# The norm's broadcasts as fp32r products of a high and a low part

## The chip, the core and the metric

The kernel runs on one core of a Trainium2 chip. The core has five engines with instruction streams of their own: PE (TensorE, matrix products, with its weight loads shown apart as PEld), DVE (VectorE), ACT (ScalarE), POOL (GpSimd) and SP (SyncE, which here only starts transfers). Each engine takes its instructions in order, and waits for another engine by semaphores. The metric is the device time of one execution in microseconds.

## The reference

One layer of three parts, on 2 batches of 768 tokens with a width of 512:

```
def _moe_ref(x, g_ln, w_ch1, w_ch2):
    mu = np.mean(x, axis=-1, keepdims=True)
    var = np.mean((x - mu) ** 2, axis=-1, keepdims=True)
    xn = (x - mu) / np.sqrt(var + 1e-06) * g_ln
    ch = np.maximum(xn @ w_ch1, 0.0) @ w_ch2
    return (x + ch).astype(np.float32)
...
def reference(**kwargs):
    attn_out = _attn_ref(**attn_kwargs)
    x = np.ascontiguousarray(attn_out.transpose(0, 2, 1, 3)).reshape(B, S, H * D)
    x = _moe_ref(x=x, **moe_kwargs)
    return _moe2_ref(x=x, **moe2_kwargs)
```

`_attn_ref` is a retention over 8 heads of 64 with a decay per head, `_moe_ref` the norm and a two-layer perceptron with 2048 hidden units, `_moe2_ref` a causal attention with 4 experts of which each token keeps two. All inputs and outputs are float32.

## The kernel before

The activations stand transposed in SBUF as `xT`: 128 partitions, 4 groups of features, 1536 tokens. The tokens are cut into 12 chunks of 128 for the retention, and into 4 blocks of 384 (`NBLK`, `TB`) for the norm and the perceptron.

**The order of the work.** PE's order is written out by hand for the whole program. Until the call `by_hand.close()` the orders of DVE, ACT, POOL and SP are written out by hand too: this stretch holds the retention, the norm, the decoding of the first eight pieces of weights and the first steps of the perceptron (the first 110 us or so). After it a scheduler with costs of its own orders the other engines.

**The hand-written loop** (L615) goes over `n`. An iteration issues, for the retention: scores of the next chunk (`sc`, PE), state and output products (`po`, PE), decay of the next chunk (`a` on DVE, `kd` on ACT and POOL), the new state (`st` on DVE, `old` on POOL), the scaled queries (`qd` on POOL) and the copy of the chunk's output into `xT` (ACT). Behind these it issues one step of the norm for each block that is ready, then a piece of decoding or of the norm (`room`), then the evictions of one perceptron step.

**The norm of a block** has five steps, one or more iterations apart.

- `ln_a`: sums over features by four fp32 products (`mu`), then a copy from PSUM to SBUF on ACT (`mus`).
- `ln_b`: an fp32 product with a matrix of constants (`mean<-mus,part_w`) adds the four part sums and gives the mean to all partitions. DVE subtracts it (`dq`, L425), ACT multiplies by the gain into the high part of `xn` (L427), DVE makes the low part (L431), ACT squares (L433).
- `ln_c`: the same sums over the squares (`va`, then `vas`).
- `ln_d`: the variance as a column per 128 tokens (`var`), ACT's square root (`std`, L459), DVE's reciprocal (`rs`, L461).
- `ln_e` and `x2_split`: `columns` gives a column of 128 values to all partitions, by a product whose stationary operand is the column repeated and whose moving operand is the identity (L448); DVE multiplies `xT` by it. `ln_e` does this for the standard deviation (`sb`), `x2_split` for its reciprocal (`rb`).

The perceptron multiplies a high and a low part: a value is written as fp32r in two tiles, and three passes (high by high, low by high, high by low) give the product. The function `split` (L200) makes such parts: ACT casts to the high part, DVE subtracts it from the source. Products in fp32r are one instruction each; an fp32 product shows as two records in the trace.

The weights come as words of 64 bit and are decoded by a chain of DVE and ACT operations per piece (L214 to L241); the last is DVE's L241, which writes the low part of `w`. A perceptron step is `h` (L485, 12 products of 384 columns), `y` (L519) or, for the first block, `yf` (L538).

Four PSUM slots of one bank (`ps_mid`) serve `mu`, `mean`, `va`, `var`, `h`, `sb` and `rb` in turn.

Of the kernel before, what the change touches and what calls it, by code (L numbers as in the profile page):

```python
# [8 lines left out]
F32 = mybir.dt.float32  # L9
F32R = mybir.dt.float32r  # L10
BF16 = mybir.dt.bfloat16
I32 = mybir.dt.int32
U32 = mybir.dt.uint32
AF = mybir.ActivationFunctionType
ALU = mybir.AluOpType
AX = mybir.AxisListType

P = 128
B, H, S, D = 2, 8, 768, 64
HP = H // 2  # L20
# [5 lines left out]
TB = 384  # L26
NBLK = B * S // TB
NTB = TB // P
# [32 lines left out]
MASKED = -1e9  # L61
# [6 lines left out]
def model(ctx, tc, qkT, kv, lam, g_ln, w12, wat, out):  # L68
    nc = tc.nc
# [4 lines left out]
    const = ctx.enter_context(tc.tile_pool(name="const", bufs=1))  # L74
# [7 lines left out]
    lnp = mp.enter_context(tc.tile_pool(name="lnp", bufs=2))  # L82
# [3 lines left out]
    rc = rp.enter_context(tc.tile_pool(name="rc", bufs=1, side="right"))  # L86
    r2 = rp.enter_context(tc.tile_pool(name="r2", bufs=2, side="right"))
# [4 lines left out]
    def ps_mid(name):  # L92
        return psum.tile([P, 512], F32, tag="mid", bufs=4, name=name)
# [1 line left out]
    ps_one = ps_mid  # L95


    zeros = const.tile([P, 512], BF16, tag="zeros", name="zeros")
    nc.vector.memset(zeros, 0.0)

    def warm(n, name):
        ps = ps_mid(f"warm{name}")
        for _ in range(n):
            nc.tensor.matmul(ps, zeros[:, :P], zeros, start=True, stop=True)

    warm(WARM[0], "a")

# [2 lines left out]
    def ret_load(b, c, part=None):  # L110
        if part != 1:
            qk = r2.tile([P, 2, HP, P], F32, tag="qk", name=f"qk{b}{c}", bufs=3)
            nc.sync.dma_start(qk, qkT[b, c])
            R[b, c] = dict(qk=qk)
        if part != 0:
            kvn = r2.tile([P, 2, H, D], F32, tag="kvn", name=f"kvn{b}{c}", bufs=3)
            nc.sync.dma_start(kvn, kv[b, c])
            R[b, c]["kvn"] = kvn
# [54 lines left out]
    while rest:  # L173
        for p in rest:
            ft, i = p
# [24 lines left out]
    def split(dst_hi, dst_lo, src):  # L200
        nc.scalar.copy(dst_hi, src)
        nc.vector.tensor_tensor(dst_lo, src, dst_hi.bitcast(F32), ALU.subtract)
# [57 lines left out]
    qpow = rc.tile([P, HP, P], F32, tag="qpow", name="qpow")  # L260
    lq = rc.tile([P, H], F32, tag="lq", name="lq")
    dec = rc.tile([P, H, P], F32, tag="dec", name="dec")
    hit = rc.tile([P, P], F32, tag="hit", name="hit")
    order = [(b, c) for b in range(B) for c in range(NC)]
    by_hand = ExitStack()
    by_hand.enter_context(tc.manual_schedule(engines={
# [23 lines left out]
                                qpow[:, :, m - 1:m].to_broadcast([P, HP, m]), ALU.mult)  # L290
        m *= 2
    sum_w = const.tile([P, 32], F32, tag="sumw", name="sum_w")
    part_w = const.tile([P, P], F32, tag="partw", name="part_w")
    eps_sb = const.tile([P, 1], F32, tag="eps", name="eps_sb")
    ident = const.tile([P, P], F32, tag="ident", name="ident")
    tri = const.tile([P, P], I32, tag="tri", name="tri")
    fill = const.tile([P, P], F32, tag="fill", name="fill")

    def constants():

        nc.gpsimd.memset(sum_w, 1.0 / DM)
        nc.gpsimd.memset(part_w, 1.0 / 32)
        nc.gpsimd.memset(eps_sb, LN_EPS)
        make_identity(nc, ident)
        nc.gpsimd.memset(fill, 0.0)
        nc.gpsimd.affine_select(fill, fill, [[-1, P]], ALU.is_ge, 1.0, base=0, channel_multiplier=1)
        nc.gpsimd.tensor_copy(tri, fill)
        nc.gpsimd.memset(fill, MASKED)

    xT = xpool.tile([P, KT, B * S], F32, tag="xT", name="xT")  # L310

# [79 lines left out]
    def ret_copy(n):  # L391
        b, c = order[n]
        r = R.pop((b, c))
        t0 = b * S + c * P
        nc.scalar.copy(xT[:, :, t0:t0 + P], r["po"][:, 0].rearrange("p (k i) -> p k i", k=KT))


    XN, LN, DQ, SCALED = {}, {}, {}, set()
    KS = (ts(0, 2), ts(2, 4))

    def ln_parts(blk, src, name):

        ps = ps_mid(f"{name}{blk}")
        for k in range(KT):
            nc.tensor.matmul(ps[k * 32:(k + 1) * 32, :TB], sum_w, src[:, k], start=True, stop=True,
                             skip_group_check=True)
        s4 = lnp.tile([P, TB], F32, tag="s4", name=f"{name}s{blk}")
        nc.scalar.copy(s4, ps[:, :TB])
        return s4

    def ln_a(blk):
        LN[blk] = ln_parts(blk, xT[:, :, blk * TB:(blk + 1) * TB], "mu")

    def ln_b(blk):

        ps = ps_mid(f"mean{blk}")
        nc.tensor.matmul(ps[:, :TB], part_w, LN[blk], start=True, stop=True)
        dq = xnp.tile([P, 2, KT, TB], F32, tag="dq", name=f"dq{blk}", bufs=1)
        sq, d = dq[:, 0], dq[:, 1]
        DQ[blk] = sq  # L420
        x = xT[:, :, blk * TB:(blk + 1) * TB]
        xn = xnp.tile([P, 2, KT, TB], F32R, tag="xn", name=f"xn{blk}")

        def minus(ks):
            nc.vector.tensor_tensor(d[:, ks], x[:, ks], ps[:, None, :TB].to_broadcast([P, 2, TB]), ALU.subtract)  # L425
            for k in range(ks.start, ks.stop):
                nc.scalar.mul(xn[:, 0, k], d[:, k], g_sb[:, k:k + 1])  # L427

        def low(ks):
            for k in range(ks.start, ks.stop):  # L430
                nc.vector.scalar_tensor_tensor(xn[:, 1, k], d[:, k], g_sb[:, k:k + 1], xn[:, 0, k].bitcast(F32),  # L431
                                               ALU.mult, ALU.subtract)
            nc.scalar.activation(sq[:, ks], d[:, ks], AF.Square)  # L433

        def ready():
            XN[blk] = xn

        return [(1.0, lambda: minus(KS[0])), (1.0, lambda: minus(KS[1])), (1.1, lambda: low(KS[0])),
                (1.1, lambda: low(KS[1])), (0.0, ready)]

    def ln_c(blk):
        LN[blk] = ln_parts(blk, DQ[blk], "va")

    def columns(col, name):

        ps = ps_mid(name)
        for c in range(NTB):
            nc.tensor.matmul(ps[:, c * P:(c + 1) * P], col[:, c:c + 1].to_broadcast([P, P]), ident,  # L448
                             start=True, stop=True, skip_group_check=True)
        return ps[:, None, :TB].to_broadcast([P, 2, TB])  # L450

    def ln_d(blk):

        ps = ps_mid(f"var{blk}")
        for c in range(NTB):
            nc.tensor.matmul(ps[:, c:c + 1], LN[blk][:, c * P:(c + 1) * P], part_w[:, :1], start=True, stop=True,
                             skip_group_check=True)
        std = lnp.tile([P, NTB], F32, tag="std", name=f"std{blk}", bufs=NBLK)
        nc.scalar.activation(std, ps[:, :NTB], AF.Sqrt, bias=eps_sb)  # L459
        rs = lnp.tile([P, NTB], F32, tag="rs", name=f"rs{blk}", bufs=NBLK)  # L460
        nc.vector.reciprocal(rs, std)  # L461
        LN[blk] = (std, rs)

    def ln_e(blk):

# [149 lines left out]
    while n < len(order) or min(norm_at) < 4 or norm_parts or weight_parts:  # L615
        if n < len(order):
            if n + 3 < len(order):
                ret_load(*order[n + 3])
            if n + 1 < len(order):
                ret_scores(n + 1)  # L620
            ret_state(n)
            ret_outer(n)
            ret_inner(n)
            if n + 1 < len(order):
                ret_decay(n + 1)
            ret_sum(n)
            if n + 1 < len(order):
                ret_qd(n + 1)
            ret_copy(n)

        for blk in range(NBLK):
            if n >= NTB * (blk + 1) and norm_at[blk] < 4 and not (norm_at[blk] == 2 and blk not in XN) \
                    and not (norm_at[blk] == 1 and blk > 0 and norm_at[blk - 1] < 3):
                norm_parts += (ln_a, ln_b, ln_c, ln_d)[norm_at[blk]](blk) or []
                norm_at[blk] += 1
        if n < len(order):
            leave = next_step(True) if n >= MLP_FROM else None
            if n < MLP_FROM:
                warm(3, f"c{n}")
            if n > 0:  # L640
                room(ROOM[leave is not None])
            if leave:
                leave()
        if n == len(order) - 1:
            rp.close()
            ap_ = ctx.enter_context(tc.tile_pool(name="ap", bufs=HX, side="right", reuse_waits="tile"))
            WPOOL2[0] = mp.enter_context(tc.tile_pool(name="wpool2", bufs=1, side="right", reuse_waits="tile"))
            weight_parts += later_parts
        if n >= len(order):
            for _ in range(2):  # L650
                leave = next_step(False)
                room(ROOM_MLP)
                if leave:
                    leave()
        n += 1
# [24 lines left out]
    while todo:  # L680
        f, args = mlp_step()
# [205 lines left out]
    for k in range(len(items) + LAG + O_AT + 1):  # L887
# [9 lines left out]
        i = k - 1  # L897
        if 0 <= i < len(items):
            att_c(*items[i])
        i = k - LAG  # L900
        if 0 <= i < len(items):
            att_t(*items[i])
        i = k - LAG - AV_AT
# [3 lines left out]
        i = k - LAG - O_AT  # L907
# [56 lines left out]
```

## Time and profile before

| what | us |
|---|---|
| median of 3 runs | 483.04 (483.02 to 484.16) |
| the profiled execution | 484.76 |
| its span, first to last instruction | 482.8 |
| PE busy in the span | 472.1 (98%) |
| DVE busy | 340.3 (70%) |
| ACT busy | 196.1 (41%) |
| POOL busy | 85.3 (18%) |

The profiled execution took 1.72 us more than the median of the runs; its span lies 2.0 us below its own time. The busy share of PE is modelled from starts, so idle time is better read from the waits and from the chain of work that ended last. That chain goes from the first instruction to the last, and names at each moment the engine that the end depended on.

### The profile page before, as it was taken

The page shows a single profiled execution, that of the slowest core. Times are in us where ns is not written, and L with a number is a line of the kernel's source. Part 1 is how long each engine was busy: PE and PEld are TensorE (multiplying, and loading weights), DVE is VectorE, ACT ScalarE, POOL GpSimd, SP SyncE. Part 2 cuts the span into 40 slices and gives each one's busy share as a digit, 9 for nine tenths or more (in the row PEclk, how much of TensorE's full clock was granted, in tenths as well). Part 3 has the DMA queues.
Part 4 walks back from the last instruction along what each step waited for, and adds up shares of the span by engine and source line. Part 5 has one row for each costly group of instructions (what it writes and reads, how often), then busy time and mean ns, then how long its engine had stood idle before and what let it go on. Part 6 is the DMA issues. An engine that isn't in the chain of part 4 may idle for free.

```text
span 482.8 us, 8791 instructions
## 1 busy us (share of the span) xinstructions
PE 472.1 (98%) x3451; PEld 437.9 (91%) x3456; DVE 340.3 (70%) x707; ACT 196.1 (41%) x447; POOL 85.3 (18%) x132
## 2 busy tenths in 40 slices
PE   8899999999999999999999999999999999999996
PEld 4667888999999999999999999999998889898885
DVE  4489688897999796923799925245579676676663
ACT  2326646622233332211233412022346575547672
POOL 5463430000000000000000000000045444334340
PEclk9899999999999999999999999999999999999999
DMA  7877511121334212310222400000000000000111
GB/s 279 331 223 240 196 45 45 45 87 45 113 107 128 90 56 77 98 34 1 87 88 87 132 0 1 1 1 1 0 2 0 24 23 22 24 2 23 45 44 67
DMA packets 10841, 35.18 MB, mean 73 GB/s; under 512 B 1456, under 2 KB 1712, under 8 KB 10800
## 3 DMA queue, kind: packets, MB, share of 16 engines
q1 hardware_dynamic: 10512, 34.49, 21.4%
q8 instruction: 27, 0.44, 0.4%
q10 hardware_dynamic: 288, 0.13, 0.1%
q14 instruction: 14, 0.11, 0.1%
HBM read 31.47 MB, written 3.15 MB: 72 GB/s over the span
## 4 chain that ended last, share of the span: by engine, by line
PE 85%; DVE 5%; issue 3%; DMA 3%; POOL 2%; ACT 1%; SPq 0%; POOLq 0%; DVEq 0%; ACTq 0%
PE h L485 27%; PE y L519 26%; PE pj L722 4%; PE s L802 4%; PE av L851 4%; PE o L872 4%; PE t L839 4%; PE pv L744 3%; PE yf L538 2%; DMA kvn<-in_kv 2%; PE po L373 1%; POOL qd L334 1%; PE sc L326 1%; PE po L366 1%; DMA qk<-in_qkT 1%
## 5 line engine op out<-in xcount | busy, mean ns | idle before, releaser
L485 PE MATMUL h<-xn,w 128*128 128x384 f32 x768 | 140.2, 336 | 0.0
L485 PEld LDWEIGHTS h<-xn,w 128*128 128x128 f32 x768 | 133.4, 188 | 2.8 <-issue 0.8
L519 PE MATMUL y<-hs,w 128*128 128x384 f32 x552 | 99.8, 334 | 0.0
L519 PEld LDWEIGHTS y<-hs,w 128*128 128x128 f32 x552 | 96.1, 188 | 0.0
L504 ACT ACTIVATE hs<-h 128x384 fp32r<-128x384 f32 x50 | 24.5, 490 | 101.7 <-PE h L485 88.3
L736 POOL TENSOR_SCALAR kh<-kh 64x384 fp32r<-64x384 f32 x16 | 8.4, 522 | 300.1 <-DVE qs L730 288.5
L505 DVE SCALAR_TENSOR_TENSOR hs<-h,hs 128x384 fp32r<-128x384 f32 x50 | 27.7, 554 | 41.1 <-ACT hs L504 41.1
L524 DVE TENSOR_TENSOR xT<-xT,y 128x768 f32<-128x768 f32 x30 | 28.5, 950 | 31.6 <-PE y L519 31.6
L829 POOL TENSOR_SCALAR att<-att,c,gw 128x128 f32<-128x128 f32 (+5 forms) x48 | 35.6, 747 | 51.8 <-DVE c L826 16.3
L229 ACT CAST w<-top 128x512 fp32r<-128x512 f32 x32 | 19.8, 620 | 52.3 <-DVE top L223 50.3
L722 PE MATMUL pj<-x,wa 128*128 128x384 f32 x192 | 35.0, 337 | 0.0
L722 PEld LDWEIGHTS pj<-x,wa 128*128 128x128 f32 x192 | 33.4, 188 | 0.0
L840 ACT COPY aT<-t 128x512 f32<-128x512 f32 (+3 forms) x64 | 26.6, 442 | 11.1 <-PE t L839 10.8
L839 PE MATMUL t<-ident,att 128*128 128x128 f32 x168 | 26.2, 275 | 0.5 <-DVE qs L730 0.5
L214 ACT ACTIVATE mag<-raw 128x512 f32<-128x512 f32 x32 | 21.2, 668 | 7.1 <-DVE w L241 7.1
L234 DVE SCALAR_TENSOR_TENSOR mag<-raw,mag 128x512 f32<-128x512 uint32 x32 | 23.2, 726 | 0.6
L851 PE MATMUL av<-aT,v 128*64 128x128 f32 x336 | 23.6, 280 | 0.0
L802 PE MATMUL s<-kh,qs 128*128 128x512 f32 (+3 forms) x64 | 23.3, 365 | 0.0
L238 DVE TENSOR_TENSOR top<-top,w 128x512 f32<-128x512 f32 x32 | 22.9, 715 | 0.0
L223 DVE SCALAR_TENSOR_TENSOR top<-raw,mag 128x512 int32<-128x512 int32 x32 | 21.9, 686 | 0.5
L241 DVE TENSOR_TENSOR w<-top,mag 128x512 fp32r<-128x512 f32 x32 | 21.9, 685 | 0.4
L851 PEld LDWEIGHTS av<-aT,v 128*64 128x64 f32 x336 | 17.8, 136 | 4.4 <-issue 3.9
(128 smaller groups left out, 726.8 us busy)
## 6 DMA issues: line engine op xcount, KB each, us to landing
raw<-in_w SPq DMA_DIRECT2D x32, 512.0 KB, 3.8
qk<-in_qkT SPq DMA_DIRECT2D x12, 512.0 KB, 5.5
kvn<-in_kv SPq DMA_DIRECT2D x12, 512.0 KB, 5.0
out<-os SPq DMA_DIRECT2D x11, 256.0 KB, 2.0
rawa<-in_wat SPq DMA_DIRECT2D x3, 512.0 KB, 3.3
rawa<-in_wat SPq DMA_DIRECT2D x1, 520.0 KB, 4.0
out<-os SPq DMA_DIRECT2D x1, 128.0 KB, 1.7
out<-os ACTq DMA_DIRECT2D x1, 128.0 KB, 1.7
```

The source lines that it names most:

```text
L234: nc.vector.scalar_tensor_tensor(mag, RAW[ft, i][:, :, 0].bitcast(U32), 2.0 ** -52, mag, ALU.mult, ALU.mult)
L485: nc.tensor.matmul(ph[:, :TB], w[:, wi, k, :], xn[:, xi, k, :], start=(i == 0), stop=(i == 11))
L504: LAST.append((nc.scalar.activation(h[:, 0], ph[:, :TB], AF.Relu), nc.vector.scalar_tensor_tensor(h[:, 1], ph[:, :TB], 0.0, h[:, 0].bitcas ...
L505: nc.vector.scalar_tensor_tensor(h[:, 1], ph[:, :TB], 0.0, h[:, 0].bitcast(F32), ALU.max, ALU.subtract)))
L519: nc.tensor.matmul(y[:, j, :TB], w[:, wi, e * P:(e + 1) * P], h[:, xi], start=(f == 0 and i == 0), stop=(f == GF - 1 and i == 2))
L524: nc.vector.tensor_tensor(xv, xv, y[:, :, :TB], ALU.add)
L722: nc.tensor.matmul(ps[:, :TB], w[:, wi, k, :], x2[:, xi, k, :], start=(i == 0), stop=(i == 11))
L802: nc.tensor.matmul(ps[:, c0:c1], q, kk[:, e, c0:c1], start=(i == 0), stop=(i == 1))
L829: nc.gpsimd.tensor_scalar(a[:, :n], a[:, :n], c, gw, ALU.mult, ALU.mult)
L839: nc.tensor.transpose(pt[:, (j - j0) * P:(j - j0 + 1) * P], a[:, j * P:(j + 1) * P], ident)
L840: nc.scalar.copy(aT[:, j0 * P:j1 * P], pt[:, :(j1 - j0) * P])
L851: nc.tensor.matmul(pav[e2 * HD:(e2 + 1) * HD, pr * P:(pr + 1) * P], v[:, j, e * HD:(e + 1) * HD], row["aT"][e][:, j * P:(j + 1) * P], star ...
```

## The change

Four things are edited.

- `ln_a` no longer copies the part sums; it splits them into a high part (ACT, L201) and a low part (DVE, L202) in fp32r, and `ln_b` adds two fp32r products with a constant matrix `part_r`.
- `ln_d` puts the standard deviation and its reciprocal side by side and splits both at once; `columns` makes two fp32r products, high and low, for each 128 tokens, with an fp32r identity `ident_r`.
- The mask and the fill value of the attention (`tri`, `fill`) are made on POOL behind the retention, in tiles of another pool; `part_w` shrinks to one column, and POOL makes `part_r` and `ident_r` instead.
- The products that keep PE busy at the start (`warm`) read one zero column repeated instead of 512 zero columns, and `hit` takes a slot of the retention's tile `a`.

```
-        s4 = lnp.tile([P, TB], F32, tag="s4", name=f"{name}s{blk}")
-        nc.scalar.copy(s4, ps[:, :TB])
-        return s4
+        return ps[:, :TB]
 
     def ln_a(blk):
-        LN[blk] = ln_parts(blk, xT[:, :, blk * TB:(blk + 1) * TB], "mu")
+        ps = ln_parts(blk, xT[:, :, blk * TB:(blk + 1) * TB], "mu")
+        LN[blk] = lnp.tile([P, 2, TB], F32R, tag="mus", name=f"mus{blk}", bufs=1)
+        split(LN[blk][:, 0], LN[blk][:, 1], ps)
...
-        nc.tensor.matmul(ps[:, :TB], part_w, LN[blk], start=True, stop=True)
+        for i in range(2):
+            nc.tensor.matmul(ps[:, :TB], part_r, LN[blk][:, i], start=(i == 0), stop=(i == 1))
...
-            nc.tensor.matmul(ps[:, c * P:(c + 1) * P], col[:, c:c + 1].to_broadcast([P, P]), ident,
-                             start=True, stop=True, skip_group_check=True)
+            for i in range(2):
+                nc.tensor.matmul(ps[:, c * P:(c + 1) * P], col[:, i, c:c + 1].to_broadcast([P, P]), ident_r,
+                                 start=(i == 0), stop=(i == 1), skip_group_check=True)
...
-        std = lnp.tile([P, NTB], F32, tag="std", name=f"std{blk}", bufs=NBLK)
-        nc.scalar.activation(std, ps[:, :NTB], AF.Sqrt, bias=eps_sb)
-        rs = lnp.tile([P, NTB], F32, tag="rs", name=f"rs{blk}", bufs=NBLK)
-        nc.vector.reciprocal(rs, std)
-        LN[blk] = (std, rs)
+        both = lnp.tile([P, 2, NTB], F32, tag="std", name=f"std{blk}")
+        nc.scalar.activation(both[:, 0], ps[:, :NTB], AF.Sqrt, bias=eps_sb)
+        nc.vector.reciprocal(both[:, 1], both[:, 0])
+        parts = lnp.tile([P, 2, 2, NTB], F32R, tag="rs", name=f"rs{blk}", bufs=NBLK)
+        split(parts[:, 0], parts[:, 1], both)
+        LN[blk] = (parts[:, :, 0], parts[:, :, 1])
...
-            nc.tensor.matmul(ps, zeros[:, :P], zeros, start=True, stop=True)
+            nc.tensor.matmul(ps, zeros, zeros[:, :1].to_broadcast([P, 512]), start=True, stop=True)
...
-    hit = rc.tile([P, P], F32, tag="hit", name="hit")
+    hit = r2.tile([P, 2, HP, P], F32, tag="a", name="hit")[:, 0, 0]
...
+            tri = ap_.tile([P, P], I32, tag="tri", name="tri", bufs=1)
+            fill = ap_.tile([P, P], F32, tag="fill", name="fill", bufs=1)
+            nc.gpsimd.memset(fill, 0.0)
+            nc.gpsimd.affine_select(fill, fill, [[-1, P]], ALU.is_ge, 1.0, base=0, channel_multiplier=1)
+            nc.gpsimd.tensor_copy(tri, fill)
+            nc.gpsimd.memset(fill, MASKED)
```

On DVE in the loop, from the variance of block 0 to the mean of block 2, the order was this:

```order
L385 TENSOR_TENSOR st_729<-po_697,old_643 128x256
L461 RECIPROCAL rs_742<-std_740 128x3
L431 SCALAR_TENSOR_TENSOR xn_658<-dq_657,g_sb,xn_658 128x384 x2
L238 TENSOR_TENSOR top_0_431<-top_0_431,w_0_590 128x512
L347 TENSOR_TENSOR a_787<-sc_748,dec 128x1024
L385 TENSOR_TENSOR st_789<-po_757,old_731 128x256
L241 TENSOR_TENSOR w_0_590<-top_0_431,mag_0_430 128x512
L218 TENSOR_SCALAR mag_0_825<-mag_0_825 128x512
```

It now is this:

```order
L383 TENSOR_TENSOR st_729<-po_697,old_642 128x256
L462 RECIPROCAL std_740<-std_740 128x3
L202 TENSOR_TENSOR rs_743<-std_740,rs_743 128x6
L430 SCALAR_TENSOR_TENSOR xn_658<-dq_657,g_sb,xn_658 128x384 x2
L238 TENSOR_TENSOR top_0_428<-top_0_428,w_0_589 128x512
L345 TENSOR_TENSOR a_789<-sc_750,dec 128x1024
L383 TENSOR_TENSOR st_791<-po_759,old_731 128x256
L202 TENSOR_TENSOR mus_810<-mu_805,mus_810 128x384
L241 TENSOR_TENSOR w_0_589<-top_0_428,mag_0_427 128x512
L218 TENSOR_SCALAR mag_0_828<-mag_0_828 128x512
```

Two subtractions (L202) are new. The first stands between the reciprocal and the low parts of `xn`, the second between the state `st` and the last decoding step of a weight (L241).

On ACT around the square root for block 0 the order was this:

```order
L459 ACT_TABLE_LOAD
L459 ACTIVATE std_740<-var_736,eps_sb 128x3
L433 ACTIVATE dq_657<-dq_657 128x768
L343 ACTIVATE kd_782<-kvn_540,dec 128x64 x3
L395 COPY xT<-po_757 128x4x128
```

It now is this:

```order
L461 ACT_TABLE_LOAD
L461 ACTIVATE std_740<-var_736,eps_sb 128x3
L201 CAST rs_743<-std_740 128x6
L432 ACTIVATE dq_657<-dq_657 128x768
L341 ACTIVATE kd_784<-kvn_597,dec 128x64 x3
L393 COPY xT<-po_759 128x4x128
```

The cast (L201) reads what DVE's reciprocal writes, and stands ahead of ACT's next square. The order of PE keeps its places; `mean` now counts 2 products instead of 1, and `sb` and `rb` 6 instead of 3.

## Rows read from the trace of the kernel before

**Rows 1.** Page, part 1: busy time, share of the span, instructions

```profile
PE 472.1 (98%) x3451; PEld 437.9 (91%) x3456; DVE 340.3 (70%) x707; ACT 196.1 (41%) x447; POOL 85.3 (18%) x132
```

**Rows 2.** Chain of waits, 34 to 62 us: start, length, what

```profile
34.86 0.86 PE mean L417 x2
...
43.81 1.45 POOL qd L334
...
57.42 1.09 PE po L366 x16
```

**Rows 3.** Chain of waits, 57 to 116 us

```profile
67.78 0.75 PE mean L417 x2
68.54 2.09 PE h L485 x12
...
100.81 0.67 PE sb L448 x6
101.48 2.11 PE yf L538 x12
...
109.83 2.08 PE yf L538 x12
```

**Rows 4.** Timeline of PE, 355.5 to 357.2 us: start, length, instruction

```profile
356.22 0.22 PE L802 MATMUL s<-kh,qs 128*128 128x128 f32 x1
...
356.50 0.27 PE L802 MATMUL s<-kl,qs 128*128 128x128 f32 x1
356.61 0.83 PE L744 MATMUL pv<-wa,x 128*128 128x260 f32 x5
```

**Rows 5.** Timeline of DVE, 31 to 50 us: in brackets idle before, and its releaser

```profile
31.73 0.99 DVE L218 TENSOR_SCALAR mag<-mag 128x512 f32<-128x512 f32 x1 [1.01 <-ACT mag L214]
35.74 1.82 DVE L425 TENSOR_TENSOR dq<-xT,mean 128x768 f32<-128x768 f32 x2 [0.16 <-PE mean L417]
49.09 1.82 DVE L425 TENSOR_TENSOR dq<-xT,mean 128x768 f32<-128x768 f32 x2 [1.12 <-PE mean L417]
```

**Rows 6.** Timeline of DVE, 57 to 78 us

```profile
57.67 0.18 DVE L461 RECIPROCAL rs<-std 128x3 f32<-128x3 f32 x1 [2.23 <-ACT std L459]
60.99 0.67 DVE L241 TENSOR_TENSOR w<-top,mag 128x512 fp32r<-128x512 f32 x1
63.04 0.64 DVE L218 TENSOR_SCALAR mag<-mag 128x512 f32<-128x512 f32 x1 [1.38 <-ACT mag L214]
63.72 1.38 DVE L219 TENSOR_SCALAR mag<-mag 128x512 int32<-128x512 int32 x1
...
69.75 0.18 DVE L461 RECIPROCAL rs<-std 128x3 f32<-128x3 f32 x1 [0.82 <-ACT std L459]
69.85 1.79 DVE L425 TENSOR_TENSOR dq<-xT,mean 128x768 f32<-128x768 f32 x2
...
77.40 0.43 DVE L219 TENSOR_SCALAR mag<-mag 128x512 int32<-128x512 int32 x1
```

**Rows 7.** Timeline of ACT and POOL, 61 to 65 us

```profile
61.95 0.50 ACT L408 COPY mus<-mu 128x384 f32<-128x384 f32 x1
62.32 0.69 ACT L214 ACTIVATE mag<-raw 128x512 f32<-128x512 f32 x1
...
62.11 2.70 POOL L334 TENSOR_TENSOR qd<-qk,qpow 128x512 f32<-128x512 f32 x2
```

**Rows 8.** Timeline of PE's weight loads, 74.4 to 77 us

```profile
75.32 0.14 PEld L405 LDWEIGHTS va<-dq,sum_w 128*32 128x32 f32 x4 [0.28 <-ACT dq L433]
```

**Rows 9.** Timeline of DVE, 108 to 111 us

```profile
108.14 0.55 DVE L505 SCALAR_TENSOR_TENSOR hs<-h,hs 128x384 fp32r<-128x384 f32 x1
108.61 0.68 DVE L241 TENSOR_TENSOR w<-top,mag 128x512 fp32r<-128x512 f32 x1
```

**Rows 10.** Groups by line and form: count, busy us, mean ns, idle before

```profile
L770 ACT ACTIVATE gw<-gw 128x12 f32<-128x12 f32 x4 | 0.8, 211 | 2.3 <-DVE gw L769 2.3
L764 DVE TENSOR_TENSOR cmp<-v 128x6 f32<-128x6 f32 x4 | 0.7, 171 | 0.1
```

More of the change, by code (lines that the diff above doesn't have):

```diff
@@ L95, in model @@
     ps_one = ps_mid
-    zeros = const.tile([P, 512], BF16, tag="zeros", name="zeros")
+    zeros = const.tile([P, P], BF16, tag="zeros", name="zeros")
     nc.vector.memset(zeros, 0.0)
@@ L292, in model @@
     sum_w = const.tile([P, 32], F32, tag="sumw", name="sum_w")
-    part_w = const.tile([P, P], F32, tag="partw", name="part_w")
+    part_w = const.tile([P, 1], F32, tag="partw", name="part_w")
     eps_sb = const.tile([P, 1], F32, tag="eps", name="eps_sb")
+    part_r = const.tile([P, P], F32R, tag="partr", name="part_r")
     ident = const.tile([P, P], F32, tag="ident", name="ident")
-    tri = const.tile([P, P], I32, tag="tri", name="tri")
-    fill = const.tile([P, P], F32, tag="fill", name="fill")
+    ident_r = const.tile([P, P], F32R, tag="identr", name="ident_r")
     def constants():
@@ L303, in constants @@
         nc.gpsimd.memset(eps_sb, LN_EPS)
+        nc.gpsimd.tensor_copy(part_r, part_w.to_broadcast([P, P]))
         make_identity(nc, ident)
[L305 to L308, printed above, removed]
+        nc.gpsimd.tensor_copy(ident_r, ident)
     xT = xpool.tile([P, KT, B * S], F32, tag="xT", name="xT")
@@ L441, in ln_c @@
     def ln_c(blk):
-        LN[blk] = ln_parts(blk, DQ[blk], "va")
+        ps = ln_parts(blk, DQ[blk], "va")
+        LN[blk] = lnp.tile([P, TB], F32, tag="vas", name=f"vas{blk}", bufs=1)
+        nc.scalar.copy(LN[blk], ps)
     def columns(col, name):
@@ L455, in ln_d @@
         for c in range(NTB):
-            nc.tensor.matmul(ps[:, c:c + 1], LN[blk][:, c * P:(c + 1) * P], part_w[:, :1], start=True, stop=True,
+            nc.tensor.matmul(ps[:, c:c + 1], LN[blk][:, c * P:(c + 1) * P], part_w, start=True, stop=True,
                              skip_group_check=True)
-        std = lnp.tile([P, NTB], F32, tag="std", name=f"std{blk}", bufs=NBLK)
-        nc.scalar.activation(std, ps[:, :NTB], AF.Sqrt, bias=eps_sb)
-        rs = lnp.tile([P, NTB], F32, tag="rs", name=f"rs{blk}", bufs=NBLK)
-        nc.vector.reciprocal(rs, std)
-        LN[blk] = (std, rs)
+        both = lnp.tile([P, 2, NTB], F32, tag="std", name=f"std{blk}")
[4 more added lines that the diff above has]
+        LN[blk] = (parts[:, :, 0], parts[:, :, 1])
     def ln_e(blk):
```

## The prediction

> **What bounds the kernel now.** I read the page first, then the chain of waits in order of time, then the timelines of DVE, ACT and POOL beside it, and last the groups by form for prices. On the page the reader is to see that PE is busy for 98% of the span [rows 1]; that alone would make each PE microsecond saved one of the kernel's. The chain shows where it holds. From 57.42 us to about 350 us it runs on PE [rows 2, 3]; before that, POOL and DVE stand in it between pieces of PE [rows 2]. Two places inside the PE stretch have almost no slack. At 75.32 us the squares of block 2 (`va`) wait 0.28 us for ACT [rows 8], and ACT's work comes from DVE's subtraction `dq` at 69.85 us, which stood behind a reciprocal that waited for the square root [rows 6]. At 109.29 us (108.61 plus 0.68) DVE finishes the low part of a weight [rows 9] that the second product of `yf` needs; `yf` is on the chain from 109.83 us [rows 3], so about 0.4 us is left when 0.17 us of draining is taken off.
>
> **What PE saves.** A `mean` costs 0.75 us [rows 3]. A product of 384 columns in fp32r costs 2.09/12 = 0.174 us (the `h` behind it [rows 3]), so the new `mean` costs 0.35 us and saves 0.40. There are four. The eight `columns` cost 0.67 us each for three fp32 products [rows 3], 0.22 apiece. The new form is two fp32r products of 128 by 128 for each. That form stands in the trace once in a row of four, in the attention: they start at 356.22 and the next group at 356.61, with 0.11 us from the last one to it [rows 4]. So the products follow each other at 0.11 us, six cost 0.66, and a `columns` saves 0.01 us, 0.1 us over all. The same four rows bound it: at (356.50 - 356.22)/3 = 0.093 us six would cost 0.56, which gives 0.9 us over all.
>
> The Trainium skill ("FP8 and Floating Point Precision", TensorE Precision Notes) says that true fp32 takes four passes through the array. By that rule two passes would replace four, and each `columns` would fall to a half of its 0.67 us, eight times 0.33 = 2.6 us in all. The rows of the attention speak against it, since a product of this shape costs as much there as half an fp32 product here; it is a rival below.
>
> **What DVE and ACT pay.** Per block, `ln_a` adds one DVE subtraction of 128x384 out of PSUM. Its like (`hs`) lasts 0.55 us and moves the next start by 0.47 [rows 9]. It also waits for ACT's cast. Per block `ln_d` adds a cast on ACT behind the reciprocal, and a subtraction on DVE behind the cast. The nearest forms are 0.21 us on ACT (12 elements) and 0.17 on DVE (6 elements) [rows 10]. Today the next DVE instruction starts 0.10 us after the reciprocal (69.75, 69.85) [rows 6]. It will start after reciprocal 0.18, hand-over, cast 0.21, hand-over, and 0.10 more. A hand-over is 0.03 (ACT's `mag` ends at 63.01 and DVE's L218 starts at 63.04 [rows 6, 7]). That makes 0.55, so 0.45 us more, on DVE and on ACT both, since the cast stands in front of ACT's next work too. Where these go:
>
> *Term A, 29 to 57 us (blocks 0 and 1 of `ln_a`, `ln_b`).* Queued behind the waiting subtraction are the decode steps, the next decay `a`, the state `st`, and through `st` POOL's `qd` and ACT's copy. But DVE idles 1.01 us in front of L218 for ACT, and 1.12 us in front of the second `dq` for `mean` [rows 5]. These waits cover the first subtraction for the most part and the second with what it pushes back. The saving of `mean` in block 1 then arrives at once: -0.4. In block 0 `dq` waited only 0.16 us for `mean` [rows 5], so DVE sets it and nothing is won. Bounds: -0.8 (both savings arrive) to +0.9 (both subtractions of 0.47 lie open). I take -0.4, since the larger idle time stands at the second.
>
> *Term B, 57 to 77 us (square roots of blocks 0 and 1, `ln_a` of block 2).* DVE and ACT run here as one chain, through `st`, ACT's copies and L218, to `dq` at 69.85 and the squares. Twice 0.45 from the roots. Between them the subtraction of block 2 waits for ACT's `mus` (61.95 to 62.45 [rows 7]), and L241, done at 60.99 before, falls behind it: the idle 1.38 us covers the wait, but 0.47 and L241's 0.67 then reach past 63.04, to 63.6. POOL's two `qd` run from 62.11 to 64.81 [rows 7], and a DVE operation that meets one is held: L219 took 1.38 us there and 0.43 at 77.40 [rows 6]. L241 now meets the first, L218 the second, L219 none, so a part of the delay comes back. I take 0.4, bounds -0.2 (DVE gets between the two `qd`) and +0.9 (one more such hold, 1.38 - 0.43). B is 0.9 + 0.4 = 1.3, from 0.7 to 1.8. The Trainium skill ("SBUF — State Buffer", Who interferes with whom) calls this an exclusive lock on a shared pair of ports, held for the whole instruction; the 1.38 us agrees with it. By it alone, with no return, the sum would be 0.2 us higher.
>
> The saving of `mean` for block 2 falls into this stretch and is worth nothing: PE waits for ACT's squares anyway [rows 8]. After it PE stands at A + B = +0.9.
>
> *Term C and D, 77 to 110 us.* `mean` of block 3 saves 0.4 on PE. DVE gets the subtraction of block 3 (0.47) and the roots of blocks 2 and 3 (0.45 each): 1.37 us. Its only longer idle times in that stretch wait for ACT work that itself follows `dq`, so nothing covers this, and the weight of 109.29 us slips by 1.37 against a slack of 0.4. PE waits there and ends 1.37 - 0.4 = 1.0 us later than it stood at 77 us, the saving of 0.4 eaten as well. Bounds: -0.4 (no wait) to +1.4.
>
> *At nothing.* POOL saves one half microsecond of constants at the start, hidden by the loads that follow; the masks run behind the retention, where POOL is idle; the zero tile is read by products that only fill a wait. From 110 us the next weights are early, so the scheduler's new order of evictions there costs nothing. Should one of these covers fail, it costs 0.3 us at most, the length of one of the operations.
>
> **The sum.** -0.4 + 1.3 + 1.0 - 0.1 = +1.8 us. On the profiled execution 484.76 + 1.8 = 486.56; its own time is 1.72 above the median of the runs, and on that median 483.04 + 1.8 = 484.84 us.
>
> **Rivals.**
> 1. *The slack holds.* Term A at its middle, B at its lower bound, and DVE in time at 109 us: -0.4 + 0.7 - 0.4 - 0.1 = -0.2, 482.8 us. For it: DVE is busy for 70% only [rows 1]. Against: the idle time lies elsewhere, and the waits of rows 6 and 8 form one chain. Not slower, so it is the case on the other side.
> 2. *The price of a product follows its columns.* At 0.174 us for 384 columns [rows 3] one of 128 would cost 0.058, six 0.35, and eight `columns` would save 8 x 0.32 = 2.6 instead of 0.1; one of the eight lies in front of 109 us and is eaten there: 1.8 - 2.6 + 0.1 + 0.3 = -0.4, 482.6 us; together with rival 1 -2.7, 480.3 us. Against it rows 4, where the shape costs 0.11. The Trainium skill's four passes (above) would bring the same.
> 3. *The queue of DVE in the retention.* The subtractions of blocks 0 and 1 lie open (A at +0.9): DVE holds `a` and `st` back, POOL's `qd` follows and PE's product at 57.42 waits. 0.9 + 1.3 + 1.0 - 0.1 = +3.1, 486.1 us. It decides from the point where the second `dq` no longer waits for `mean`.
>
> **How the numbers follow.** About 0.3% (1.45 us) is what a measurement here can tell from no change. Chances: forecast 0.50 with its own range 484.0 to 485.5 (two thirds of it beyond the bound), rival 1 0.22, rival 2 0.10 (half of it faster), rival 3 0.18. Slower: 0.34 + 0.17 = 0.51. Faster: 0.05 + 0.02 = 0.07. The same: 0.42. Range 482.3 to 486.2: it leaves out the lowest of rivals 1 and 2 and the end of rival 3.
>
> **What would show it.** In the profile after: `mean` at 0.35 us and `sb` at 0.66 for six products; the cast between `std` and the square on ACT, with DVE waiting for it; the wait of `va` for ACT's squares longer than 0.28; a wait of `yf` for L241 near 110 us of about 1 us; PE's product of 57.42 us earlier by some tenths. The prediction is wrong if `sb` falls to 0.35, if `yf` doesn't wait, or if `dq` of block 2 comes as early as before.

## The result, and the profile after

The changed kernel takes 485.9 us (median of 4, 485.7 to 486.2), the kernel before 483.03 us (median of 4, 482.76 to 484.16). The ratio is 1.0059, with a 95% interval of 1.0045 to 1.0072: slower by 2.9 us. The forecast was 484.8 us with a range of 482.3 to 486.2 us. Its direction is right and the time lies in the range, though near its upper end and beyond the 484.0 to 485.5 us given to the forecast itself; a term of 1.2 us is missing in the sum.

**A common start first.** The profiled execution of before took 484.76 us, that of after 486.01 us. That difference, 1.25 us, is too small, because the executions don't begin alike. The view of stretches shows it: busy time by engine between 18 and 23 us, then the granted clock, the DMA share and GB/s. Before:

```profile
18.00:23.00 5.00, 3.97 (x46) 3.66 (x48) 3.34 (x4) 1.47 (x5) 1.59 (x2) 0.66 0.77 305
```

After:

```profile
18.00:23.00 5.00, 4.12 (x66) 3.46 (x67) 3.42 (x5) 1.34 (x4) 1.46 (x2) 1.00 0.76 303
```

In the execution of before TensorE was granted 0.66 of its clock in the mean here (a part of the stretch at 1.2 GHz, the rest at 2.4) and began 46 products instead of 66. In both executions PE had stood idle for 1.87 us just ahead, for a load; only before did the clock then fall. The state `st` that DVE writes at 28.02 us after (first row of the next view) came at 29.69 us before, ahead of anything that the norm's edits touch. Before:

```profile
29.69 0.42 DVE L385 TENSOR_TENSOR st<-po,old 128x256 f32<-128x256 f32 x1 [0.60 <-PE po L373]
```

In this section and below I count from that row: S is the start of this `st`, M the first `h` product behind the `yf` that waits near 109 us, L the last of the 1488 products of `h` and `y`. The run's time less S is 455.07 us before and 457.99 us after: 2.92 us, which is what the medians say (2.87).

**From S to M: +1.48 us.** DVE of after, from 28 to 71 us, with the idle time before an instruction and what ended it in brackets. These rows answer to [rows 5, 6].

```profile
28.02 0.42 DVE L383 TENSOR_TENSOR st<-po,old 128x256 f32<-128x256 f32 x1 [0.60 <-PE po L371]
29.48 0.56 DVE L202 TENSOR_TENSOR mus<-mu,mus 128x384 fp32r<-128x384 f32 x1 [1.03 <-ACT mus L201]
...
42.23 0.56 DVE L202 TENSOR_TENSOR mus<-mu,mus 128x384 fp32r<-128x384 f32 x1 [1.03 <-ACT mus L201]
...
55.30 0.18 DVE L462 RECIPROCAL std<-std 128x3 f32<-128x3 f32 x1 [2.23 <-ACT std L461]
55.74 0.17 DVE L202 TENSOR_TENSOR rs<-std,rs 128x6 fp32r<-128x6 f32 x1 [0.26 <-ACT rs L201]
55.83 1.14 DVE L430 SCALAR_TENSOR_TENSOR xn<-dq,g_sb,xn 128x384 fp32r<-128x384 f32 x2
...
60.45 0.56 DVE L202 TENSOR_TENSOR mus<-mu,mus 128x384 fp32r<-128x384 f32 x1 [1.42 <-ACT mus L201]
60.92 0.68 DVE L241 TENSOR_TENSOR w<-top,mag 128x512 fp32r<-128x512 f32 x1
61.52 1.49 DVE L218 TENSOR_SCALAR mag<-mag 128x512 f32<-128x512 f32 x1
...
68.14 0.18 DVE L462 RECIPROCAL std<-std 128x3 f32<-128x3 f32 x1 [0.82 <-ACT std L461]
68.58 0.17 DVE L202 TENSOR_TENSOR rs<-std,rs 128x6 fp32r<-128x6 f32 x1 [0.26 <-ACT rs L201]
68.66 1.81 DVE L424 TENSOR_TENSOR dq<-xT,mean 128x768 f32<-128x768 f32 x2
```

Read as distances from S: the reciprocal of block 0 stands 27.98 us behind `st` before (57.67 - 29.69) and 27.28 after, so 0.70 is won up to there. Only 0.30 of it is the shorter `mean`: from the start of `mean` of block 1 to that of the `sc` behind its `h` it is 2.94 us before and 2.64 after. The other 0.40 is there before this `mean` starts, at the `po` product that waits for POOL's `qd` (15.62 behind S before, 15.22 after). POOL of before, then of after:

```profile
42.91 0.94 POOL L389 TENSOR_TENSOR old<-st,qpow 128x256 f32<-128x256 f32 x1 [2.55 <-PE mu L405]
43.81 1.45 POOL L334 TENSOR_TENSOR qd<-qk,qpow 128x512 f32<-128x512 f32 x1
```

```profile
41.34 0.62 POOL L387 TENSOR_TENSOR old<-st,qpow 128x256 f32<-128x256 f32 x1 [2.55 <-DVE st L381]
41.92 1.27 POOL L332 TENSOR_TENSOR qd<-qk,qpow 128x512 f32<-128x512 f32 x1
```

While DVE waits for ACT ahead of the subtraction at 42.23, POOL's two operations take 0.62 and 1.27 us instead of 0.94 and 1.45 (that this wait is the reason is read from the times alone). The `po` stands at 15.20 to 15.23 behind S in six of the seven profiles of the table below with the mean of blocks 0 and 1 in two parts (the seventh, with 64 bytes empty, has a delay of its own), and at 15.62 to 15.63 in the five with an fp32 mean.

The `dq` of block 2 stands at 40.16 before and at 40.64 after, 0.48 late, so 1.18 is lost between the two. The next start of DVE behind a reciprocal comes 0.53 us later (55.30, 55.83), where it was 0.10 [rows 6]: 0.43 more for each root. L218 now meets POOL's `qd` and takes 1.49 us. POOL of after:

```profile
59.69 3.04 POOL L332 TENSOR_TENSOR qd<-qk,qpow 128x512 f32<-128x512 f32 x2
```

At the end of the stretch PE waits for the weight, as [rows 9] let one expect. PE of after:

```profile
108.25 0.34 PE L541 MATMUL yf<-hs,w 128*128 128x384 f32 x1
109.55 2.18 PE L541 MATMUL yf<-hs,w 128*128 128x384 f32 x11 [0.96 <-DVE w L241]
111.56 2.25 PE L488 MATMUL h<-xn,w 128*128 128x384 f32 x12
```

The weight is the one that DVE's L241 finishes:

```profile
108.82 0.68 DVE L241 TENSOR_TENSOR w<-top,mag 128x512 fp32r<-128x512 f32 x1
```

The chain of waits, which ran on PE there before [rows 3], runs on DVE from 97 us on and comes back to PE with this `yf`:

```profile
97.33 0.69 DVE w L241
...
108.90 0.61 DVE w L241
109.50 0.04 issue
109.55 2.18 PE yf L541 x11
111.73 2.09 PE h L488 x12
113.81 0.62 PE sb L450 x6
```

**From M to L: +1.22 us, where nothing was predicted.** PE is never idle there, neither before nor after; its steps are longer. The chain of before from 212 to 224 us, then that of after:

```profile
211.94 4.16 PE h L485 x24
216.10 4.16 PE y L519 x24
220.26 4.16 PE h L485 x24
```

```profile
212.04 4.24 PE h L488 x24
216.28 4.24 PE y L522 x24
220.52 4.16 PE h L488 x24
```

4.16 us for 24 products is 173.3 ns from start to start, 4.24 is 176.7 ns. The slow steps take their weights from the second pool (`wpool2`), and the `h` at 220.52 us takes them from the first. Over the 432 products of the normed blocks `xn` and the hidden blocks `hs` with weights of that pool, the mean of the trace's start-to-start times is 173.5 ns before and 176.3 after: 432 x 2.8 = 1.21 us, which is the whole of it. From L to the end it is 142.09 us before and 142.30 after.

### The profile page after: what moved, and what is told of

Same layout as the page of the kernel before. It is cut to its first block, busy times and chain, and to the rows that moved or that the text cites. A ratio compares the mean times of both kernels' runs of the same rounds, so it can differ in the third digit from the quotient of the medians.

```text
span 484.1 us, 8804 instructions
## 1 busy us (share of the span) xinstructions
PE 470.8 (97%) x3456; PEld 436.7 (90%) x3456; DVE 342.5 (71%) x715; ACT 196.5 (41%) x451; POOL 85.7 (18%) x134
## 4 chain that ended last, share of the span: by engine, by line
PE 71%; DVE 6%; ACT 2%; issue 1%; POOL 0%; DVEq 0%; ACTq 0%
PE y L522 26%; PE h L488 21%; PE pj L731 4%; PE s L811 4%; PE av L860 4%; PE o L881 4%; PE t L848 4%; PE pv L753 3%; DVE qs L739 1%; ACT att L823 1%; PE rb L450 1%; DVE kl L743 0%; PE yf L541 0%; DVE w L241 0%; DVE negm L814 0%
## 5 line engine op out<-in xcount | busy, mean ns | idle before, releaser
L241 DVE TENSOR_TENSOR w<-top,mag 128x512 fp32r<-128x512 f32 x32 | 22.2, 695 | 0.4
```

## The experiments

The table puts all profiled executions beside each other, in us, from the starts of the records of PE and of `st`. "Pitch" is the mean start-to-start time of the 432 products named above. The two columns on places are the addresses in a partition, modulo 64 bytes, of the normed and hidden blocks, and of the second pool's weights, in the built program. The medians of before, measured again beside each group of runs, lie between 482.95 and 483.07 us.

| kernel | median | S to M | M to L | L to end | blocks | pool 2 | pitch, ns |
|---|---|---|---|---|---|---|---|
| before | 483.03 | 82.06 | 230.92 | 142.09 | 32 | 32 | 173.5 |
| before, profiled again | (482.11) | 82.04 | 230.92 | 142.07 | 32 | 32 | 173.5 |
| before, 32 bytes empty | 484.48 | 82.16 | 232.16 | 142.14 | 0 | 32 | 176.3 |
| room alone | 484.35 | 82.14 | 232.16 | 141.86 | 0 | 32 | 176.3 |
| mean alone | 484.43 | 81.86 | 232.16 | 142.31 | 0 | 32 | 176.3 |
| columns alone | 485.66 | 83.37 | 232.14 | 142.44 | 0 | 32 | 176.3 |
| after | 485.9 | 83.54 | 232.14 | 142.30 | 0 | 32 | 176.3 |
| after, 64 bytes empty | 486.48 | 84.10 | 232.36 | 142.52 | 0 | 32 | 176.6 |
| after, roots split on DVE | 485.65 | 83.50 | 232.14 | 142.03 | 0 | 32 | 176.3 |
| after, 32 bytes empty | 485.05 | 83.52 | 231.07 | 142.44 | 32 | 32 | 173.4 |
| after, 32 bytes behind the masks | 484.89 | 83.54 | 231.12 | 142.20 | 0 | 0 | 173.4 |
| two means | 482.8 | 81.38 | 231.08 | 142.29 | 32 | 32 | 173.4 |

### Room alone

The norm is that of before; the zero tile, `hit`, the masks and the small constants are those of after. `ones_w`, the old constant matrix, stands in another pool, behind the places in question.

```
-        LN[blk] = lnp.tile([P, 2, TB], F32R, tag="mus", name=f"mus{blk}", bufs=1)
-        split(LN[blk][:, 0], LN[blk][:, 1], ps)
+        LN[blk] = lnp.tile([P, TB], F32, tag="mus", name=f"mus{blk}", bufs=1)
+        nc.scalar.copy(LN[blk], ps)
...
-        for i in range(2):
-            nc.tensor.matmul(ps[:, :TB], part_r, LN[blk][:, i], start=(i == 0), stop=(i == 1))
+        nc.tensor.matmul(ps[:, :TB], ones_w, LN[blk], start=True, stop=True)
...
-            for i in range(2):
-                nc.tensor.matmul(ps[:, c * P:(c + 1) * P], col[:, i, c:c + 1].to_broadcast([P, P]), ident_r,
-                                 start=(i == 0), stop=(i == 1), skip_group_check=True)
+            for _ in range(1):
+                nc.tensor.matmul(ps[:, c * P:(c + 1) * P], col[:, c:c + 1].to_broadcast([P, P]), ident,
+                                 start=True, stop=True, skip_group_check=True)
...
-        parts = lnp.tile([P, 2, 2, NTB], F32R, tag="rs", name=f"rs{blk}", bufs=NBLK)
-        split(parts[:, 0], parts[:, 1], both)
-        LN[blk] = (parts[:, :, 0], parts[:, :, 1])
+        LN[blk] = (both[:, 0], both[:, 1])
```

> The norm as in the kernel before (fp32 mean and columns, no parts); every other edit of the change stays: the zero tile of 128 columns, hit on a tile of the retention, the masks made behind the retention, the smaller constants. With them every tile behind the constants lies 1248 bytes lower in a partition, and the weights of the second pool 1024 bytes lower. Theory P (placement): the products of the weights of the second pool run at 176.6 ns instead of 173.3 here as in the changed kernel, since only the places in memory decide it; +1.1 us from 140 to 292 us, 484.1 us on a median of 483.0. Theory N (the norm's timing shifts ACT, DVE or the loads against PE, and that slows the products): 173.3 ns in all steps, 483.0 us, the same as before.

484.35 us (7 runs) against 482.95; ratio 1.0026 (1.0015 to 1.0038). M to L is that of after to 0.02 us, S to M that of before to 0.1. The norm's timing has nothing to do with the slower products; the room edits alone bring them. Its chain shows the same two lengths as that of after:

```profile
210.64 4.24 PE h L487 x24
214.88 4.24 PE y L521 x24
219.12 4.16 PE h L487 x24
```

### 32 bytes left empty, in the changed kernel

```
     eps_sb = const.tile([P, 1], F32, tag="eps", name="eps_sb")
+    const.tile([P, 8], F32, tag="pad", name="pad")
```

> The changed kernel with 32 bytes a partition left empty among the constants, so that the normed blocks and the weights of the first pool lie 32 bytes higher and again at 32 modulo 64 as in the kernel before; the weights of the second pool stay. Theory P: what counts is where the weights of the second pool lie against the normed blocks modulo 64 bytes (equal before, 32 apart after); the products return to 173.3 ns, 485.9 - 1.1 = 484.8 us. Theory N: the pad changes nothing, 176.6 ns and 485.9 us.

485.05 us (5 runs), 0.85 below the changed kernel, against a before of 482.95; ratio to before 1.0045 (1.0033 to 1.0058). The pitch is back at 173.4 ns and M to L falls by 1.07 us, with an S to M of 83.52 (after: 83.54). The chain, the first two of these steps:

```profile
211.77 4.16 PE h L489 x24
215.93 4.16 PE y L523 x24
```

### The same 32 bytes in the kernel before, and on the other side of the changed one

The first has the pad line above in the kernel before. The second has it behind the masks, so that only the second pool moves:

```
             fill = ap_.tile([P, P], F32, tag="fill", name="fill", bufs=1)
+            ap_.tile([P, 8], F32, tag="pad", name="pad", bufs=1)
```

> The kernel before with 32 bytes a partition left empty among the constants, nothing else: the normed blocks, the hidden blocks and the weights of the first pool move from 32 to 0 modulo 64 bytes, and the weights of the second pool stay at 32. Theory P (products are slow where the weight and the block it multiplies lie 32 bytes apart modulo 64): products with weights of the second pool at 176.3 ns instead of 173.3 from about 140 to 292 us, +1.2 us, 484.2 us. Rival (what slows them is the move of the second pool by 1024 bytes or of the others by 1248, not the 32 bytes): 173.3 ns, 483.0 us.

> The changed kernel with 32 bytes a partition left empty behind the masks, so that the weights of the second pool move from 32 to 0 modulo 64 bytes, where the normed blocks, the hidden blocks and the first pool lie already. Theory P: equal places modulo 64 again, 173.3 ns, 485.0 us as with the 32 bytes on the other side. Rival (it is the blocks at 0 modulo 64 that are read slowly beside the second pool, wherever its weights lie): 176.3 ns, 485.9 us.

The pad makes the kernel before slower: 484.48 us (6 runs) against 482.99, ratio 1.0030 (1.0019 to 1.0042), M to L 232.16. No instruction differs. On the other side it makes the changed kernel faster: 484.89 us (5 runs), ratio 1.0036 (1.0022 to 1.0050), M to L 231.12, although the blocks lie at 0 modulo 64 as in the changed kernel. So it is not the blocks' own place that counts but the weights' place against theirs. Before with the 32 bytes:

```profile
210.55 4.24 PE h L486 x24
214.79 4.24 PE y L520 x24
```

### 64 bytes

The pad of the changed kernel with `[P, 16]`.

> The changed kernel with 64 bytes a partition left empty among the constants instead of 32: the normed blocks and the first pool move by 64 bytes and lie at 0 modulo 64 as without the pad, the second pool at 32. Theory P (the place modulo 64 decides): 176.3 ns stays and the kernel takes 485.9 us. Rival (any move of that size brings the 173.3 ns back, or the place counts modulo 128): 173.4 ns and 485.0 us.

486.48 us (5 runs), ratio 1.0069 (1.0055 to 1.0083); pitch 176.6 ns, M to L 232.36. A move of 64 bytes brings nothing back, a move of 32 does. The kernel is 0.6 us slower than expected. In the profiled execution, which took 487.06 us, 0.56 us more than in after stands from S to M (84.10 against 83.54) and 0.22 in each of the two later stretches. From S to M the reason is another than the place of the weights. DVE and POOL of the changed kernel, near 32 us:

```profile
32.37 0.43 DVE L219 TENSOR_SCALAR mag<-mag 128x512 int32<-128x512 int32 x1
```

```profile
32.42 0.97 POOL L342 TENSOR_TENSOR kd<-kvn,dec 128x320 f32<-128x320 f32 x1 [0.36 <-DMA kvn<-in_kv]
```

The same two with the 64 bytes:

```profile
32.41 0.99 DVE L219 TENSOR_SCALAR mag<-mag 128x512 int32<-128x512 int32 x1
```

```profile
32.39 0.73 POOL L343 TENSOR_TENSOR kd<-kvn,dec 128x320 f32<-128x320 f32 x1 [0.30 <-DMA kvn<-in_kv]
```

Where DVE starts 0.05 us ahead of POOL it takes 0.43 us, where it starts 0.02 behind, 0.99: the 0.56 us by which S to M is longer. (The first `dq` behind it stands 0.56 later from S, 6.72 against 6.16.) The Trainium skill ("SBUF — State Buffer", Who interferes with whom) says that whichever of the two issues first holds the shared ports for its whole instruction; these four rows agree with that.

### Mean alone, columns alone

Each is the changed kernel with the other half of the norm put back to fp32 by the lines shown under room alone.

> The changed kernel with only the mean in two parts; std and 1/std go back to fp32 products, and neither root is split. Theory C (the two handed-over instructions behind each root delay the chain of DVE and ACT by 0.45 us four times, and the subtraction of the mean adds 0.5 in the second stretch): 29 to 57 us stays at -0.7; 57 to 77 us falls from +1.2 to +0.3; at 109 us the delay is +0.1 or less and the mean of block 3 saves 0.4 until then; 485.9 - 1.8 = 484.1 us, all of the rest being the placement. Rival (the subtractions of the mean, held by POOL's lock on the port, are what costs): 485.4 us, with dq of block 2 still 1.0 us late.

> The changed kernel with std and 1/std in two parts, and the mean in fp32 as before (copied by ACT). Theory C: 29 to 57 us gives nothing (0.0 instead of -0.7); 57 to 77 us +0.9 for two roots; at 109 us two more roots, 0.9 against a slack of 0.4; with +1.1 for the placement 483.0 + 0.9 + 0.5 + 1.1 = 485.5 us. Rival (the subtractions of the mean are what costs): 57 to 77 us at most +0.3, and 484.2 us.

Mean alone: 484.43 us (5 runs), ratio 1.0032 (1.0019 to 1.0045). Columns alone: 485.66 us (5 runs), 1.0060 (1.0047 to 1.0073). Against room alone (484.35), whose room is the same, the mean costs 0.1 us, which is inside the scatter, and the columns 1.3. Theory C had 484.1 and 485.5 us, the rivals 485.4 and 484.2. From S to M the mean wins 0.28 and the columns lose 1.23. The sum of both would be 83.09; after has 83.54. What adds up is DVE's delay of the awaited weight (L241 near 109 us, from S, against room alone): 0.18 us by the mean, 1.70 by the columns, 1.88 in after. The 1.70 are about four roots at 0.43. In after, what the mean wins on PE is lost again in the wait for that weight. Mean alone, DVE: behind a reciprocal the next instruction starts after 0.10 us again.

```profile
67.81 0.18 DVE L462 RECIPROCAL std<-std 128x3 f32<-128x3 f32 x1 [0.81 <-ACT std L461]
67.91 1.79 DVE L424 TENSOR_TENSOR dq<-xT,mean 128x768 f32<-128x768 f32 x2
```

From S, `dq` of block 2 stands here at 39.87 (67.91 - 28.04), in after at 40.64. Columns alone shows the same 0.77 us against before (40.93 and 40.16). So 0.77 of the 1.18 us that are lost between the first reciprocal and this `dq` belong to the two roots, and the other 0.41 to the subtraction of block 2 and the POOL instruction that it pushes DVE into. The rival that put the cost on the subtractions falls.

### Roots split on DVE

```
-        split(parts[:, 0], parts[:, 1], both)
+        nc.vector.tensor_copy(parts[:, 0], both)
+        nc.vector.tensor_tensor(parts[:, 1], both, parts[:, 0].bitcast(F32), ALU.subtract)
```

> The changed kernel with the parts of std and 1/std both made on DVE (a copy and a subtraction behind the reciprocal), so that DVE hands nothing to ACT and waits for nothing there. Theory C: the next start of DVE behind a root comes 0.26 us after the reciprocal instead of 0.53, 0.26 less four times, on the chain: 485.9 - 1.0 = 484.9 us. Rival (what costs is ACT's late cast, not DVE's wait, or the waits are hidden): 485.7 to 485.9 us.

485.65 us (5 runs), ratio 1.0055 (1.0043 to 1.0068): 0.25 us below after, not 1.0, and S to M is the same to 0.04. My expectation was wrong. DVE:

```profile
55.34 0.18 DVE L462 RECIPROCAL std<-std 128x3 f32<-128x3 f32 x1 [2.23 <-ACT std L461]
55.55 0.20 DVE L464 CAST rs<-std 128x6 fp32r<-128x6 f32 x1
55.79 0.17 DVE L465 TENSOR_TENSOR rs<-std,rs 128x6 fp32r<-128x6 f32 x1
55.87 1.14 DVE L430 SCALAR_TENSOR_TENSOR xn<-dq,g_sb,xn 128x384 fp32r<-128x384 f32 x2
```

An instruction that reads what the one before it on DVE wrote starts 0.21 and 0.24 us behind it here, while the next, which doesn't, starts after 0.08. Two dependent steps on DVE take 0.45 us (55.34 to 55.79), the way over ACT 0.44 (55.30 to 55.74). The hand-over wasn't the price; the chain of three dependent small instructions is.

### Two means

Blocks 0 and 1 have the mean in two parts, all else of the norm is fp32, and the room is that of after with the 32 bytes.

```
-        split(LN[blk][:, 0], LN[blk][:, 1], ps)
...
+        if blk < 2:
+            split(LN[blk][:, 0], LN[blk][:, 1], ps)
+        else:
+            nc.scalar.copy(LN[blk][:, 0], ps)
```

> Blocks 0 and 1 broadcast their mean in two parts; the means of blocks 2 and 3 and all std and 1/std stay fp32 as before; the room as in the changed kernel with the 32 bytes among the constants. Theory C: the 0.70 us of 29 to 57 us are kept, nothing is added behind them, products at 173.3 ns: 483.0 - 0.7 = 482.3 us, faster than both. Rival (the 0.70 is taken back by another wait in front of 110 us, or the products stay slow): 483.0 us or more.

482.80 us (11 runs) against 482.99, ratio 0.9999 (0.9989 to 1.0009): 3.1 us below the changed kernel, and no difference from before that can be measured. The 482.3 us of the expectation was missed. S to M is 0.68 below before, as expected. Of that, 0.16 is lost again from M to L and 0.20 from L to the end, where twelve profiles scatter between 141.86 and 142.52 us.

### The kernel before, profiled again

> The kernel before once more, unchanged, for a profile. If the 1.7 us by which its first profiled execution lies above the median come from the half clock of TensorE between 18 and 22 us, a profile without that stretch shows st at 28.0 us instead of 29.7, every later step 1.7 us earlier, and a time of 483.0 us. Rival (the profiled execution is 1.7 us slower for another reason, as by the profiling itself): st at 28.0 or 29.7 us, and 484.7 us either way.

One run of 482.11 us, with `st` at 27.08 us and the granted clock at 1.00 from 18 to 23 us. Both expectations missed the start by 0.9 us and the time with it: the start differs between executions even without the half clock. From S on the run agrees with the first profile to 0.04 us (455.03 and 455.07), and that is what the comparison needs.

## Why the prediction was right and where it was wrong

**Term A** was -0.4 and measured -0.70, in its bounds, and in part by luck. The wait for ACT in front of the two subtractions is 1.03 us each time (rows at 29.48 and 42.23): the idle time of [rows 5] took them up, as argued, and in block 0 nothing is won (`dq` is 0.11 later from S). `dq` no longer waits for `mean` in either block. The `mean` of block 1 saves 0.30 us and not 0.40, counted from starts; the further 0.40 comes from POOL's `old` and `qd`, which run shorter while DVE waits, and for that the prediction had no term.

**Term B** was +1.3 and measured +1.18: the two roots 0.77 (predicted 0.9) and block 2 0.41 (predicted 0.4), with the hold by POOL at L218 in place of L219, as foretold.

**Terms C and D** were 1.37 us more on DVE against 0.4 of slack. L241 of the awaited weight starts 78.92 us behind `st` before and 80.80 after (108.82 - 28.02): 1.88 late, of which 0.48 stood at `dq` of block 2, so 1.40 come from here. PE's M is 1.48 late, so the slack was 0.40. The wait of `yf` is 0.96 us; about 1 was foretold. From S to M the terms give -0.4 + 1.3 + 1.0 = 1.9, and 1.48 was measured; the difference of 0.4 is 0.3 of term A and 0.1 of term B.

**The columns** were put at 0.1 us for eight. `sb` takes 0.62 for six products in the chain, near the price from [rows 4], where 0.67 stood; but from six products ahead of a `columns` to six behind it the starts lie 2.58 to 2.61 us apart in room alone and in after (the last of the eight has another neighbour, and 2.31 in both), so nothing is saved. Rival 2 (0.35) is out, and the four passes of the Trainium skill ("FP8 and Floating Point Precision", TensorE Precision Notes) do not show as time in this shape. M to L is no shorter with the new columns (232.14) than without (232.16).

**The step that failed** is the one that costed room edits at nothing and "0.3 us at most" should a cover fail, "the length of one of the operations". It asked what the edits issue and not what they move. The smaller constants put the blocks 1248 bytes lower, and the masks in their new pool put the second pool 1024 bytes lower. Modulo 64 the blocks moved by 32 bytes and the second pool by none, and that slowed 432 products of PE. That is 1.22 of the 2.92 us, on the engine that [rows 1] show at 98%, so nothing could hide it. The runs with 32 bytes show the cause from both sides, and the run with 64 bytes shows that it is not any move.

**The rest** is 0.2 us from L to the end, no more than the scatter there. The miss of the forecast is 485.9 - 484.8 = 1.1 us: +1.22 for the products, +0.2 for the end, -0.3 for the norm. That the time still lies in the range is luck: it reaches beyond the forecast's own 485.5 us for the sake of rival 3. With the 32 bytes that take the slow products away the changed kernel took 484.89 and 485.05 us, in the forecast's own range.

Rival 1 fell with the wait of `yf`. Rival 3 named 486.1 us, close to the time, but by a mechanism that isn't there: the first reciprocal came 0.70 us earlier, not later. The point from which it was to decide, a second `dq` that no longer waits for `mean`, was reached, and still PE's product of 57.42 us came 0.69 us earlier from S. Without the room's part the change costs about 1.5 us (after stands 2.87 above its before, room alone 1.40), nearly all by the roots' parts.

## What to carry to other kernels

- Splitting a small operand so that PE can run fp32r products puts dependent small instructions into DVE's chain, 0.43 us each time here; here it won time only where DVE was waiting anyway, as in blocks 0 and 1, and where the product is long (0.30 us for the `mean` of 384 columns, nothing for the products of 128).
- When a change resizes tiles, compare the addresses of the two operands of the long products before and after, and in the trace the start-to-start time of equal steps; an engine that is busy all the time can still have become slower.
- Line two traces up on a row ahead of the change before subtracting: here the starts differed by 1.7 us.

## What the runs showed of the hardware that was not expected

Products of 384 fp32r columns follow each other at 173.4 to 173.5 ns where weight and block lie equally modulo 64 bytes in their partitions, and at 176.3 to 176.6 ns in the mean where they lie 32 bytes apart, in this kernel's second pool: five profiles with 32 and 32 or 0 and 0, seven with 0 and 32. In the changed kernel all 23 steps of such an unequal pair from 141.8 us on run at 176.6 to 176.9 ns; of those between 114 and 141 us some run at 173.3, and the `hx` and `hw` blocks don't follow the rule cleanly (24 products of `hx` with first-pool weights took 176.2 ns in before and 173.5 in the changed kernel with 32 bytes, at equal places both times). So the mechanism stays open. The Trainium skill ("SBUF — State Buffer", Who interferes with whom) gives PE independent ports for the moving block and the weights and says that PE never waits on anyone. By that one would not expect the two places to matter to each other; the measurement differs.
